# Mask added by TensorE for all head pairs, and P transposed by two transfers a pair

## The chip, the cores and the metric

The kernel runs on one core of a Trainium2 chip. The core has a matrix engine (TensorE, PE in the profile), three engines that work on elements (VectorE or DVE, ScalarE or ACT, GpSimd or POOL) and SyncE (SP), which here only issues transfers. All of them run side by side; each works through its own list of instructions in order, and an instruction starts when the semaphores it waits for have been raised. Matmul results land in PSUM, in banks of 128 x 512 numbers of 32 bits; everything else lies in SBUF, 128 partitions wide. The metric is the time of one execution on the device in microseconds; less is better.

## The reference

An attention with a forgetting gate is followed by a gated feed-forward network (FFN). There are 8 batches and 8 heads, 576 tokens, head size 64; the FFN takes 4608 tokens of 512 numbers to 1536 and back.

```python
scores = q @ k.T / sqrt(64)                       # per batch and head, 576 x 576
cum    = cumsum(log(clip(f, 1e-4, 1)))            # per batch and head, 576
scores = where(j > i, -1e9, scores + cum[i] - cum[j])
attn   = softmax(scores) @ v
x      = attn, heads side by side                 # 4608 x 512
out    = (silu(x @ w_gate) * (x @ w_val)) @ w_out
```

Since `cum[i]` is the same for a whole row, the softmax does not need it. The kernel computes `t = cum[j] - q.k/8` and takes `exp(min(t) - t)`; a masked place needs a very large `t`.

## The kernel before, in words

**Tiling.** The two heads of a pair are worked on together; there are 32 pairs, 0 to 31, four to a batch. A pair's 576 queries are cut into nine blocks of 64, and block `i` of both heads fills the 128 partitions (`qz` holds the queries with zeros in the other head's half). Block `i` sees only keys 0 to 64(i+1), so its row has 64(i+1) columns. Blocks 0 to 3 are group `g = 0`, blocks 4 to 8 group `g = 1`. The score rows are packed into banks (`BANKS`): two for group 0, five for group 1. A unit of work is a pair and a group.

**Stages of a unit.** (1) `load_pair` loads k, q and `cb` (the row `cum` of each head, spread over 64 partitions), `prepare` casts k and q on GpSimd, transposes them on TensorE (L447) and copies them out of PSUM (L459, L461). (2) `scores` multiplies a bank's rows on TensorE (L493) into one of two PSUM buffers `sp`. (3) VectorE adds `cb` to a row and writes `t`, and takes the least of the row in the same instruction; a second small instruction reads that least out into `tm` (all L517). (4) ScalarE takes the exponential with its row sum (L532). (5) VectorE turns row sums into factors `lr` (L546 to L550), GpSimd multiplies each row by its factor and packs it as 16-bit slices of 128 keys into `pk` (L568): 6 slices for group 0 and 19 for group 1. (6) The slices are transposed into `pT`. For pairs 0 to 7 (`ON_PE`) TensorE does that (L598), with copies out of PSUM (L603); for pairs 8 on, one transposing transfer issued by SyncE (L581) takes all 25 slices when both groups are packed (`joint`). (7) `weighted` multiplies by v on TensorE (L624); from pair 8 on it does both groups at once and waits for both halves of `pT`. The result is copied into `xT` (L648).

**The mask.** Only the last 64 columns of a row (the block against its own keys) need a mask. For pairs below `MFROM = 12`, TensorE adds it: one more matmul of 64 columns a row adds `mask` through the identity into the score bank (L497). For pairs 12 on, a copy `cm = cb + mask` of a pair is made first by GpSimd or VectorE (L476), and a row's add on VectorE is split in two: the earlier columns with `cb`, the last 64 with `cm`. The second piece starts from the least of the first, which it reads from `tm`.

**The FFN.** Tokens are cut into tiles 0 to 11 of 256, 256, seven times 512, 256, 128 and 128. `gate` multiplies by the two input matrices on TensorE (L706), ScalarE takes a tanh (L712), VectorE makes the product (L714, L717); `project` multiplies by the output matrix (L734), ScalarE or VectorE copies (L741, L743), SyncE stores (L746). In four PSUM buffers `gv` the FFN shares space with the transposes of P.

**What sets the order.** `Plan.order` goes through all operations before the program is written: each has costs by engine, what it reads and writes, and a priority. At each step the operation that can start first by these costs is placed on an engine, ties going to the lower priority number. So the costs, the latencies, the number of buffers in each pool, and the priorities fix the order of each engine's list; nothing is reordered at run time except what the engines do themselves. Attention units have low numbers (`at[p, g]`, the place in `ORDER`), the FFN's matmuls 1000 and more, so FFN work goes where attention cannot start. `NUDGE` adds to the priority of single units: `a` a unit of attention, `q` the preparation of a pair, `v` a batch's v, `f` and `o` a tile's gate and projection. `WAIT` makes an operation count as starting later by so many ns. SyncE's list holds all loads, transposing transfers and stores in that order, so one that waits holds up those behind it.

Of the kernel before, what the change touches and what calls it, by code (L numbers as in the profile page):

```python
# [14 lines left out]
BIG = 1.0e9  # L15
HUGE = 3.0e38
COLD = 25000


class Op:  # L20
# [11 lines left out]
class Plan:  # L32
# [29 lines left out]
    def order(self):  # L62
# [72 lines left out]
        while ready:  # L135
            best = None
            for n, r in ready.items():
                o = self.ops[n]
                got = room(o, r)
                if got is None:  # L140
                    continue
                for e, dur in o.engs.items():
                    s = max(r, got[0], free[e])
                    for k in o.reads:
                        if k in using and using[k][0] != e:
                            s = max(s, using[k][1])
                    c = (s + o.bias.get(e, 0), o.prio, n, e, dur, got[1])
                    if best is None or c[:4] < best[:4]:
                        best = c
            if best is None:  # L150
                raise RuntimeError("no operation can start: " + ", ".join(str(self.ops[n].writes) for n in list(ready)[:20]))
            s, _, n, e, dur, take = best
            o = self.ops[n]
            s -= o.bias.get(e, 0)
            if e == "PE" and s < COLD:
                dur *= 2
            for k, b in take:
                name = self.home[k]
                self.where[k] = b
                slots[name][b] = k  # L160
                taken[name, self.line[k]] += 1
            o.start, o.eng = s, e
            free[e] = s + dur
            for k in o.reads:
                if self.home.get(k) in self.banks:
                    using[k] = e, s + dur + 30
            if o.dma:
                q = e == "POOL"
                at = max(wire[q], s + (2550 if q else 2000))
                both = max(0, min(2 * o.dma, wire[not q] - at))  # L170
                wire[q] = at + o.dma + both / 2
                wire[not q] += both / 2
                if o.ring:
                    free[e] = max(free[e], wire[q] - 1450)
                o.end = wire[q] + 1100
            else:
                o.end = free[e] + o.lat
            for k in {*o.writes, *o.reads, *o.holds}:
                left[k] -= 1
                until[k] = max(until[k], o.end)  # L180
            del ready[n]
            for kid in kids.get(n, ()):
                waiting[kid.n] -= 1
                if not waiting[kid.n]:
                    ready[kid.n] = max(d.end for d in kid.deps)
            done.append(o)
# [10 lines left out]
def kernel(  # L197
# [36 lines left out]
             [[(8, 0, 512)], [(8, 512, 576), (6, 0, 448)], [(7, 0, 512)], [(5, 0, 384)], [(4, 0, 320)]]]  # L234


    MFROM = 12
    CMENG = ("POOL", "DVE")

    ON_PE = {(p, g) for p in range(8) for g in range(2)}  # L240

    NDIRECT = 0
    NSEL = 1
    MOST = (("p", 1), ("o", 2), ("f", 3))
# [11 lines left out]
    HEAD = "10 00 20 30 11 01 31 21"  # L256


    NUDGE = "a21.0:1 a31.1:10 f5:1 f7:4.5 o8:2 q11:-2 q15:4 q24:2.5"

    WAIT = ""
    ORDER = [(int(u[0]), int(u[1])) for u in HEAD.split()]
    ORDER += [(p, g) for p in range(len(ORDER) // 2, NPAIR) for g in (1, 0)]
    at = {u: n for n, u in enumerate(ORDER)}
# [30 lines left out]
    for i in range(0, NB, 2):  # L295
        bufs(f"e{i}", [P, QB * (i + 2)], F32, 2)
    bufs("eo", [P, 512], F32, 4)
    bufs("tm", [P, NB + 1], F32, 6)
    bufs("ls", [P, NB, 2], F32, 6)
    bufs("lr", [P, NB], F32, 6)  # L300
    both = {}
    for n in ("pk", "pT"):
        both[n] = [sb.tile([P, sum(NSL), P], BF16, name=f"{n}{x}") for x in range(2)]
# [114 lines left out]
    def prepare(p):  # L418
        s = first[p]
        for name in ("k", "q"):  # L420
# [4 lines left out]
            def cast(e, name=name, fk=fk, bk=bk, KR=KR):  # L425
# [5 lines left out]
                    eng[e].tensor_scalar(dst, src, -scale, 1.0, op0=ALU.mult, op1=ALU.mult)  # L431
                else:
                    eng[e].tensor_copy(dst, src)
            engs = {"POOL": 850}
            if p < NPB:
                engs = {"POOL": 850, "ACT": 850, "DVE": 500} if name == "k" else {"POOL": 1050, "ACT": 1050, "DVE": 680}
            o = pl.op(engs, cast, [fk], [bk], s - 1 + (name == "q") * .1)
# [30 lines left out]
    def copies(p):  # L468

        if p < MFROM:  # L470
            return
        pl.key(("cm", p), "cm")

        def add(e):
            src = pl.buf(("cb", p)).rearrange("r (i c) -> r i c", c=QB)
            eng[e].tensor_tensor(pl.buf(("cm", p)), src, maskf.unsqueeze(1).to_broadcast((P, NB, QB)), op=ALU.add)  # L476
        cost = {"POOL": S * 1.05 + 245, "DVE": S / .96 + 82}
        pl.op({e: cost[e] for e in CMENG}, add, [(("cb", p), 3)], [("cm", p)], first[p] - .5, holds=[("cb", p)])

    def scores(p, g):  # L480
        s = at[p, g]
        pl.key(("tm", p, g), "tm")
        pl.key(("ls", p, g), "ls")
        for n, bank in enumerate(BANKS[g]):
            sk = ("sp", p, g, n)
            pl.key(sk, "sp")
            pr = s + n * .05

            def mult(e, bank=bank, sk=sk):
                sp, kt, qz, o = pl.buf(sk), pl.buf(("kt", p)), pl.buf(("qz", p)), 0  # L490
                for i, a, z in bank:
                    last = z == QB * (i + 1)
                    nc.tensor.matmul(sp[:, o:o + z - a], qz[:, i, :, :].rearrange("p h r -> p (h r)"), kt[:, a:z],  # L493
                                     start=True, stop=not last or p >= MFROM)
                    o += z - a
                    if last and p < MFROM:
                        nc.tensor.matmul(sp[:, o - QB:o], ident, mask, start=False, stop=True)  # L497
            cols = [z - a for _, a, z in bank] + [64 for i, a, z in bank if z == QB * (i + 1) and p < MFROM]
            pl.op({"PE": mm(*cols)}, mult, [("kt", p), ("qz", p), (("kt", p), "done"), (("qz", p), "done"), "mask"], [sk], pr, lat=220)
            o = 0  # L500
            cuts = []
            for i, a, z in bank:
                last = z == QB * (i + 1)
                if last and a < QB * i and p >= MFROM:
                    cuts += [(i, a, QB * i), (i, QB * i, z)]
                else:
                    cuts.append((i, a, z))
            for i, a, z in cuts:
                last = z == QB * (i + 1)
                own = last and p >= MFROM  # L510
                tk = ("t", p, i)
                if a == 0:
                    pl.key(tk, "t")

                def add(e, i=i, a=a, z=z, o=o, sk=sk, tk=tk, last=last, own=own):
                    tm = pl.buf(("tm", p, g))
                    nc.vector.tensor_tensor_reduce(  # L517
                        out=pl.buf(tk)[:, a:z], in0=pl.buf(sk)[:, o:o + z - a],
                        in1=pl.buf(("cm", p))[:, i, :] if own else pl.buf(("cb", p))[:, a:z], scale=1.0,
                        scalar=HUGE if a == 0 else tm[:, NB:NB + 1], op0=ALU.add, op1=ALU.min,  # L520
                        accum_out=tm[:, i:i + 1] if last else tm[:, NB:NB + 1])
                w = [tk, ("tm", p, g)] + ([("m", p, i)] if last else [("m", p, i, "part")])
                r = [sk] + ([("cm", p)] if own else [(("cb", p), 3)]) + ([("m", p, i, "part")] if a else [])
                pl.op({"DVE": (z - a) / .96 + (142 if a else 82)}, add, r, w, pr, lat=100, holds=[] if own else [("cb", p)])
                o += z - a
                if last:
                    ek = ("e", p, i)
                    pl.key(ek, epool(i))

                    def exp(e, i=i, tk=tk, ek=ek):  # L530
                        L = QB * (i + 1)
                        nc.scalar.activation(pl.buf(ek)[:, :L], pl.buf(tk)[:, :L], AF.Exp,  # L532
                                             bias=pl.buf(("tm", p, g))[:, i:i + 1], scale=-1.0,
                                             accum_out=pl.buf(("ls", p, g))[:, i, 0:1])
                    sums[p, g] = pl.op({"ACT": QB * (i + 1) * .833 + 290}, exp, [tk, ("m", p, i)], [ek, ("ls", p, g)],
                          pr, lat=150, holds=[("tm", p, g)])

    def normalize(p, g):
# [10 lines left out]
        pl.op({"DVE": 95, "ACT": 200}, guard, [("ls", p, g)] + ([("z", "ls", n) for n in range(6)] if p < 3 else []), [("lr", p, g)], s, lat=120)  # L549
        pl.op({"DVE": 95}, lambda e: nc.vector.reciprocal(lr(), lr()), [("lr", p, g)], [("l2", p, g)], s, lat=170, holds=[("lr", p, g)])  # L550
        kk = ("pk", p, g)
        joint = not any((p, x) in ON_PE for x in range(2))
        pl.key(kk, f"pk{g}", same=("pk", p, 1 - g) if joint else None)
        w = HI[g] - LO[g] + 1
        for i in range(HI[g], LO[g] - 1, -1):
# [75 lines left out]
    def spread(p, g, pv):  # L631
# [5 lines left out]
        for a, z in ((0, cut), (cut, w)):  # L637
# [3 lines left out]
            def evac(e, a=a, z=z):  # L641
# [5 lines left out]
                src = bass.AP(src.tensor, src.offset + QB * (z - a - 1), [full[0], [-QB, z - a], full[2]])  # L647
                (nc.scalar.copy if e == "ACT" else nc.vector.tensor_copy)(dst, src)  # L648
            tok = t0 + a * QB, t0 + z * QB
            o = pl.op({"ACT": QB * (z - a) * .833 + 130, "DVE": QB * (z - a) / .96 + 85}, evac, [xk],  # L650
                      [("x", hp, n) for n in range(tok[0] // QB, tok[1] // QB)], s)
            o.bias = LATER if p >= 8 else {}
            evacs.append((pv, tok))
# [1 line left out]
    def load_v(b):  # L655
        for c in range(5):
# [9 lines left out]
                (), [fk], s, dma=1460 if n == P else 800, after=wait)  # L666
            def cast(e, c=c, n=n, fk=fk):
                (nc.scalar.copy if e == "ACT" else eng[e].tensor_copy)(pl.buf(("vt", b))[0:n, c, :, :], pl.buf(fk)[0:n, :, :])
            o = pl.op({"POOL": 670} if b else {"POOL": 670, "ACT": 580, "DVE": 600}, cast,
                  [fk] + ([("z", "vt", b)] if c == 4 and b < 2 else []), [("vt", b), ("vt", b, c)], s + .5)  # L670
            o.bias = SPARE

# [183 lines left out]
```

## Time and profile before

| | |
|---|---|
| median of 3 runs | 425.94 us (425.29 to 428.68) |
| profiled execution | 422.99 us |
| its span, first to last instruction | 421.1 us |
| granted TensorE clock | 1.000 |
| TensorE busy in the first 40 us, and from 400 to 420 us | 24.56 us, 17.87 us |
| transfers | 72.21 MB, mean 171 GB/s |

The profile gives, for one execution, each engine's busy time, the same in 40 equal slices, the chain of work that ended last, the costliest groups of instructions by source line, and who waited for whom. A busy TensorE is not the same as a TensorE at its peak: matmuls are pipelined, so one that shows as 0.38 us long can be followed by the next after 0.22 us. What counts is the distance from start to start. "Idle before" names what ended an idle time; it counts from the modelled end of the instruction before.

### The profile page before, as it was taken

How to read it: one execution, taken by the hardware profiler on the slowest of the kernel's cores; microseconds unless marked ns; L12 is line 12 of the kernel's file. 1: busy time of each engine (PE TensorE's matmuls, PEld its weight loads, DVE VectorE, ACT ScalarE, POOL GpSimd, SP SyncE). 2: the span in 40 equal slices, each digit the busy share in tenths (PEclk: the TensorE clock that was granted, in tenths of full speed). 3: DMA queues.
4: the chain of work that ended last, by engine and by line, in shares of the span. 5: the costliest groups of instructions: out<-in, count | busy, mean ns of one | idle time of the engine just before them, and what ended most of it. 6: DMA issues, size and time to landing. Idle time of an engine off the chain costs nothing.

```text
span 421.1 us, 10007 instructions
## 1 busy us (share of the span) xinstructions
PE 397.9 (94%) x3124; PEld 226.6 (54%) x3124; DVE 349.9 (83%) x1329; ACT 318.6 (76%) x882; POOL 269.3 (64%) x468
## 2 busy tenths in 40 slices
PE   2579999999999999999999999999999999999996
PEld 1446888665555555444544455454544444457675
DVE  4699999989998999899998999899989972765132
ACT  4599999999987989878998898798897843332221
POOL 7399978999985968767798696777964630000000
PEclk9999999999999999999999999999999999999999
DMA  7999999997999999999897999989948234000121
GB/s 199 197 151 248 213 213 208 230 233 181 203 205 198 262 189 225 225 247 190 175 228 187 235 208 214 221 193 188 224 113 166 57 85 115 2 25 27 51 76 50
DMA packets 143029, 72.21 MB, mean 171 GB/s; under 512 B 117760, under 2 KB 129792, under 8 KB 142976
## 3 DMA queue, kind: packets, MB, share of 16 engines
q1 hardware_dynamic: 136804, 66.27, 72.4%
q0 software_dynamic: 5808, 4.72, 7.5%
q10 hardware_dynamic: 364, 0.59, 0.5%
q8 instruction: 24, 0.39, 0.4%
q14 instruction: 29, 0.24, 0.2%
HBM read 47.04 MB, written 9.58 MB: 134 GB/s over the span
## 4 chain that ended last, share of the span: by engine, by line
PE 65%; DVE 18%; ACT 4%; issue 4%; DMA 4%; POOL 3%; SPq 0%; DVEq 0%; ACTq 0%; POOLq 0%
PE gv L706 33%; PE gv L734 16%; DVE t L517 10%; PE sp L493 7%; PE tx L624 4%; DMA qf<-in_q_dram 3%; DVE th L714 3%; PE tx L447 3%; DVE hh L717 3%; PE gv L598 2%; POOL pk L568 2%; ACT e L532 1%; ACT eo L532 1%; DVE qz L461 1%; DVE tm L517 1%
## 5 line engine op out<-in xcount | busy, mean ns | idle before, releaser
L568 POOL TENSOR_SCALAR pk<-e,lr 128x512 bf16<-128x512 f32 (+3 forms) x190 | 104.3, 552 | 55.6 <-issue 15.5
L517 DVE CUSTOM_DVE_ANT_0 t<-sp,cb 128x320 f32<-128x320 f32 (+7 forms) x268 | 121.0, 461 | 12.8 <-PE sp L493 1.7
L706 PE MATMUL gv<-xT,wv 128*128 128x512 bf16 (+2 forms) x576 | 111.2, 326 | 0.7 <-DVE th L714 0.6
L706 PE MATMUL gv<-xT,wg 128*128 128x512 bf16 (+2 forms) x576 | 111.4, 326 | 0.0
L734 PE MATMUL gv<-wo,hh 128*128 128x512 bf16 (+1 forms) x444 | 105.2, 373 | 0.0
L532 ACT ACTIVATE e<-t,tm 128x64 f32<-128x64 f32 (+4 forms) x160 | 88.6, 555 | 10.5 <-DVE tm L517 9.8
L714 DVE SCALAR_TENSOR_TENSOR th<-th,gv 128x512 f32<-128x512 f32 x108 | 73.8, 683 | 26.5 <-ACT th L712 25.8
L712 ACT ACTIVATE th<-gv 128x512 f32<-128x512 f32 x108 | 63.6, 590 | 32.5 <-PE gv L706 30.9
L532 ACT ACTIVATE eo<-t,tm 128x256 f32<-128x256 f32 (+3 forms) x128 | 71.3, 558 | 15.5 <-DVE tm L517 13.4
L493 PE MATMUL sp<-kt,qz 128*128 128x448 bf16 (+4 forms) x320 | 73.3, 293 | 6.6 <-DVE tm L517 5.8
L717 DVE TENSOR_TENSOR hh<-th,gv 128x512 bf16<-128x512 f32 x108 | 73.8, 684 | 4.2 <-PE gv L706 1.3
L568 POOL TENSOR_SCALAR pk<-eo,lr 128x256 bf16<-128x256 f32 (+3 forms) x128 | 68.2, 533 | 6.7 <-DVE tm L517 3.3
L706 PEld LDWEIGHTS <-wv 128*128 128x128 bf16 x576 | 50.6, 98 | 38.1 <-issue 3.6
L706 PEld LDWEIGHTS <-wg 128*128 128x128 bf16 x576 | 50.4, 98 | 36.8 <-issue 0.6
L734 PEld LDWEIGHTS <-hh 128*128 128x128 bf16 x444 | 41.0, 98 | 40.2 <-issue 1.0
L493 PEld LDWEIGHTS <-qz 128*128 128x128 bf16 x320 | 30.6, 100 | 27.3 <-issue 5.2
L517 DVE CUSTOM_DVE_ANT_0 t<-sp,cm,tm 128x64 f32<-128x64 f32 x160 | 42.2, 278 | 2.1 <-PE sp L493 0.2
L741 ACT ACTIVATE ot<-gv 128x512 f32<-128x512 f32 (+1 forms) x33 | 19.0, 578 | 25.5 <-PE gv L734 25.0
L517 DVE DVE_READ_ACCUMULATOR2_ANT tm<- 128x1 f32 x460 | 38.1, 83 | 0.0
L431 POOL TENSOR_SCALAR qb<-qf 72x1024 bf16<-72x1024 f32 x30 | 31.2, 1040 | 6.2 <-DMA qf<-in_q_dram 5.3
L459 ACT COPY qz<-tx 64x576 bf16<-64x576 bf16 x46 | 28.9, 628 | 3.5 <-PE tx L447 3.0
L532 ACT ACTIVATION_READ_ACCUMULATOR e<-t,tm 128x1 f32 x160 | 30.5, 191 | 0.0
(64 smaller groups left out, 403.1 us busy)
## 6 DMA issues: line engine op xcount, KB each, us to landing
out_dram<-ot SPq DMA_DIRECT2D x35, 256.0 KB
kf<-in_k_dram SPq DMA_DIRECT2D x31, 288.0 KB
qf<-in_q_dram SPq DMA_DIRECT2D x31, 288.0 KB
cb<-cum_f SPq DMA_DIRECT2D x62, 144.0 KB
vf<-in_v_dram SPq DMA_DIRECT2D x32, 256.0 KB
wo<-in_moe_w_out_dram POOLq DMA_DIRECT2D x3, 512.0 KB, 10.8
vf<-in_v_dram SPq DMA_DIRECT2D x8, 128.0 KB
wv<-in_moe_w_val_dram POOLq DMA_DIRECT2D x2, 512.0 KB, 7.6
```

The lines of the kernel that those rows point to most:

```text
L431: eng[e].tensor_scalar(dst, src, -scale, 1.0, op0=ALU.mult, op1=ALU.mult)
L459: nc.scalar.copy(dst, src)
L493: nc.tensor.matmul(sp[:, o:o + z - a], qz[:, i, :, :].rearrange("p h r -> p (h r)"), kt[:, a:z], start=True, stop=not last or p >= MFROM)
L517: nc.vector.tensor_tensor_reduce(out=pl.buf(tk)[:, a:z], in0=pl.buf(sk)[:, o:o + z - a], in1=pl.buf(("cm", p))[:, i, :] if own else pl.buf ...
L532: nc.scalar.activation(pl.buf(ek)[:, :L], pl.buf(tk)[:, :L], AF.Exp, bias=pl.buf(("tm", p, g))[:, i:i + 1], scale=-1.0, accum_out=pl.buf(( ...
L568: eng[e].tensor_scalar(dst, src, r, 1.0, op0=ALU.mult, op1=ALU.mult)
L706: nc.tensor.matmul(pl.buf(bk)[:, j * n:j * n + n], wt[:, ko, fc * P:fc * P + P], xT[:, ko, x0:x0 + n], start=ko == 0, stop=ko == KD - 1)
L712: pl.op({"ACT": 487}, lambda e, u=u: nc.scalar.activation(pl.buf(("th", t, u)), pl.buf(("wg", t, u)), AF.Tanh, scale=0.5), [("wg", t, u)], ...
L714: pl.op({"DVE": 605}, lambda e, u=u: nc.vector.scalar_tensor_tensor(pl.buf(("th", t, u)), pl.buf(("th", t, u)), 1.0, pl.buf(("wg", t, u)), ...
L717: pl.op({"DVE": 605}, lambda e, u=u: nc.vector.tensor_mul(pl.buf(("hh", t, u)), pl.buf(("th", t, u)), pl.buf(("wv", t, u))), [("u", t, u), ...
L734: nc.tensor.matmul(pl.buf(bk)[:, 0:z - a], hh[:, (fc % nf) * n + ms * P:(fc % nf) * n + ms * P + P], wo[:, fc, a:z], start=fc == 0, stop=f ...
L741: nc.scalar.mul(pl.buf(ok)[:, a:z], pl.buf(bk)[:, 0:z - a], 0.5)
```

## The change

`MFROM` goes from 12 to 32, so all pairs add their mask on TensorE: `cm` is never built, and no row is split at its last 64 columns. `JFROM = 32` takes the place of the test on `ON_PE`: no pair is joint any more, and from pair 8 on each group has a transposing transfer of its own, of 19 and of 6 slices. `lr` has 5 buffers in place of 6. `tm` has another layout, with the same content for these pairs. Several costs by which the order is planned are set anew (VectorE's by 3% after 100 us of the plan, GpSimd's casts, ScalarE's copies, a latency), and `NUDGE` and `WAIT` name more units. With `TWO` a branch is added that pairs from `MFROM` on would take; with `MFROM = 32` no pair takes it. `HEAD`, the order of the first units, stays.

```diff
 COLD = 25000
+SLOW = 1.03
...
             if e == "PE" and s < COLD:
                 dur *= 2
+            if e == "DVE" and s > 100000:
+                dur *= SLOW
...
-    MFROM = 12
+    MFROM = 32
...
+    JFROM = 32
+    TWO = True
...
-    NUDGE = "a21.0:1 a31.1:10 f5:1 f7:4.5 o8:2 q11:-2 q15:4 q24:2.5"
-
-    WAIT = ""
+    NUDGE = "a11.0:1 a12.0:1.5 a14.0:0.5 a15.0:-0.5 a15.1:0.5 a16.0:2 a17.0:-0.5 a19.0:-2.5 a21.0:1 a22.0:-2 a23.0:2 a24.1:4 a25.0:-2 a26.0:2 a28.1:2 a31.1:10 f5:1 f7:8.5 f9:-7 o8:2 o9:-1 q11:-2 q15:3 q24:2.5 q25:-0.5 v6:10.5 v7:12"
+
+    WAIT = "f8:200"
...
-    bufs("tm", [P, NB + 1], F32, 6)
+    bufs("tm", [P, 2, NB], F32, 6)
     bufs("ls", [P, NB, 2], F32, 6)
-    bufs("lr", [P, NB], F32, 6)
+    bufs("lr", [P, NB], F32, 5)
...
-            engs = {"POOL": 850}
+            engs = {"POOL": 850 if p < 8 else 800 if name == "k" else 1010}
...
-                pl.op({"DVE": (z - a) / .96 + (142 if a else 82)}, add, r, w, pr, lat=100, holds=[] if own else [("cb", p)])
+                pl.op({"DVE": (z - a) / .96 + (142 if a and not two else 82)}, add, r, w, pr, lat=100 if p < 8 else 140, holds=[] if own else [("cb", p)])
...
-        joint = not any((p, x) in ON_PE for x in range(2))
+        joint = p >= JFROM
...
-            o = pl.op({"ACT": QB * (z - a) * .833 + 130, "DVE": QB * (z - a) / .96 + 85}, evac, [xk],
+            o = pl.op({"ACT": QB * (z - a) * .833 + (130 if p < 8 else 50), "DVE": QB * (z - a) / .96 + 85}, evac, [xk],
...
-            o = pl.op({"POOL": 670} if b else {"POOL": 670, "ACT": 580, "DVE": 600}, cast,
+            o = pl.op({"POOL": 670 if b < 2 else 590} if b else {"POOL": 670, "ACT": 580, "DVE": 600}, cast,
```

With `joint` false, a pair from 8 on takes this branch, which the kernel before has too and did not use:

```python
        if (p, g) not in ON_PE:
            pl.op({"SP": 300 + 153 * NSL[g]}, lambda e: nc.sync.dma_start_transpose(
                out=pl.buf(tk), in_=pl.buf(kk).rearrange("p s k -> p (s k)")),
                [kk], [tk], s - 1, dma=500 + 118 * NSL[g]).ring = True
            return
```

## The prediction

> **What bounds the kernel now.** I read the page first, then the busy time by stretch, the chain, and the waits of TensorE.
>
> ```profile
> span 421.1 us, 10007 instructions
> ...
> PE 397.9 (94%) x3124; PEld 226.6 (54%) x3124; DVE 349.9 (83%) x1329; ACT 318.6 (76%) x882; POOL 269.3 (64%) x468
> ...
> PE   2579999999999999999999999999999999999996
> ...
> DVE  4699999989998999899998999899989972765132
> ...
> PEclk9999999999999999999999999999999999999999
> ```
>
> ```profile
> 0.00:40.00 40.00, 24.56 (x222) 17.63 (x223) 29.03 (x108) 29.10 (x81) 29.62 (x73) 1.00 1.00 196
> 40.00:120.00 80.00, 79.52 (x841) 54.83 (x839) 77.22 (x266) 77.56 (x217) 72.43 (x120) 1.00 1.05 214
> 120.00:340.00 220.00, 215.93 (x1487) 107.21 (x1484) 205.58 (x900) 187.58 (x542) 163.70 (x271) 1.00 0.93 196
> 340.00:418.00 78.00, 77.87 (x582) 46.96 (x580) 38.03 (x58) 24.04 (x45) 3.51 (x6) 1.00 0.15 47
> ```
>
> In the second view the columns after the stretch and its length are busy time of PE, PEld, DVE, ACT and POOL. Two engines look full from 40 to 340 us: TensorE and VectorE. They are not full in the same way. VectorE stops mattering at 340 us; TensorE goes on without a hole to the end. The chain says how:
>
> ```profile
> 343.93 6.91 PE gv L734 x32
> 350.83 0.81 PE tx L624 x14
> ...
> 355.20 17.27 PE gv L706 x80
> ```
>
> 32 matmuls of 512 columns in 6.91 us, 80 in 17.27: one takes a **slot** of 0.216 us (0.42 ns a column and little more), back to back. So what is done earlier shortens the last stretch, and what is added on TensorE anywhere lengthens the span by its slot. The kernel's time is the start, plus TensorE's slots, plus TensorE's holes. VectorE matters only through the holes:
>
> ```profile
> PE sp L493 <- DVE tm L517: 2.0, 8, 0.4
> PE gv L706 <- DVE th L714: 0.6, 2, 0.3
> PE tx L447 <- ACT xT L648: 0.4, 1, 0.4
> PE tx L447 <- POOL qb L431: 0.4, 1, 0.4
> ```
>
> These are TensorE's waits from 120 to 345 us: scores wait until VectorE has emptied one of the two score banks. They understate the loss, because a matmul's modelled end hides the start of a hole:
>
> ```profile
> 284.05 1.03 PE L706 MATMUL gv<-xT,wg 128*128 128x512 bf16 x4
> 285.48 0.38 PE L493 MATMUL sp<-kt,qz 128*128 128x512 bf16 x1 [0.41 <-DVE tm L517]
> ```
>
> Four slots from 284.05 end at 284.91; the score starts at 285.48. The hole is 0.57 us, of which 0.41 is shown: 0.16 is hidden.
>
> **How large are the holes where the change acts?** From below: 220 - 215.93 = 4.07 us idle, plus 0.16 for each of the 12 waits, 6.0 us. From above I count slots from 120 to 340 us; these are the first four and the last of 18 rows by shape:
>
> ```profile
> L706 PE MATMUL gv<-xT,wg 128*128 128x512 bf16 x243 | 62.6, 379 | 0.0
> L706 PE MATMUL gv<-xT,wv 128*128 128x512 bf16 x240 | 61.6, 379 | 0.6 <-DVE th L714 0.6
> L734 PE MATMUL gv<-wo,hh 128*128 128x512 bf16 x240 | 59.6, 379 | 0.0
> L493 PE MATMUL sp<-kt,qz 128*128 128x512 bf16 x40 | 15.2, 379 | 0.8 <-DVE tm L517 0.4
> ...
> L624 PE MATMUL tx<-pT,vt 128*64 128x64 bf16 x44 | 4.3, 193 | 0.0
> ```
>
> 763 matmuls of 512 columns x 0.216 = 164.8; 22 weighted groups (44 matmuls of 64 columns, two a group) x 0.81 from the chain = 17.8; smaller scores by their columns 15.9, transposes of k and q 9.4. Together 207.9, so 12.1 us at most are holes. I take 9, midway.
>
> **Mask on TensorE for pairs 12 to 31.** By the order of instructions this adds 180 mask matmuls (108 become 288), each with a weight load. Masked pairs stand in the trace already:
>
> ```profile
> 112.16 0.19 PE L497 MATMUL sp<-mask,ident 128*128 128x64 bf16 x1
> 112.18 0.35 PE L493 MATMUL sp<-kt,qz 128*128 128x448 bf16 x1
> 112.37 0.19 PE L497 MATMUL sp<-mask,ident 128*128 128x64 bf16 x1
> 112.40 1.03 PE L706 MATMUL gv<-xT,wv 128*128 128x512 bf16 x4
> ...
> L497 PEld LDWEIGHTS <-ident 128*128 128x128 bf16 x108 | 10.6, 103 | 6.1 <-issue 3.7
> ```
>
> A mask starts, and the next matmul starts 0.02 to 0.03 us later; it shows 0.19 because of its tail. At 0.029 (64 columns), 180 cost **5.2 us**, all on the path. The 0.10 us weight loads vanish in neighbouring slots.
>
> The Trainium skill speaks against this price. "TensorE: Matmul & The Clock Gate", section "Back-to-back issue gap", says that in a stream of weight loads and matmuls a 128-column matmul is spaced at about 81 ns, since columns alone leave out the load. By that figure 180 masks would be an estimated 14.6 us. The trace, with 0.03 us between starts, disagrees here.
>
> On VectorE 140 split adds go, each with its accumulator read (460 reads become 320), and 12 builds of the masked copy; on GpSimd 8 builds:
>
> ```profile
> L517 DVE CUSTOM_DVE_ANT_0 t<-sp,cm,tm 128x64 f32<-128x64 f32 x160 | 42.2, 278 | 2.1 <-PE sp L493 0.2
> ...
> L517 DVE CUSTOM_DVE_ANT_0 t<-sp,cb 128x512 f32<-128x512 f32 x44 | 30.0, 681 | 0.1
> ...
> L517 DVE CUSTOM_DVE_ANT_0 t<-sp,cb 128x448 f32<-128x448 f32 x32 | 19.8, 617 | 1.7 <-ACT lr L546 0.2
> ...
> L476 POOL TENSOR_TENSOR cm<-cb,maskf 128x576 f32<-128x576 f32 x8 | 11.3, 1409 | 0.0
> ...
> L476 DVE TENSOR_TENSOR cm<-cb,maskf 128x576 f32<-128x576 f32 x12 | 10.3, 859 | 0.2
> ...
> 284.05 0.28 DVE L517 CUSTOM_DVE_ANT_0 t<-sp,cm,tm 128x64 f32<-128x64 f32 x1
> 284.26 0.08 DVE L517 DVE_READ_ACCUMULATOR2_ANT tm<- 128x1 f32 x1
> 284.26 0.16 DVE L548 TENSOR_REDUCE lr<-ls 128x5 f32<-128x10 f32 x1
> ```
>
> A split add holds VectorE from 284.05 to 284.26, 0.21 us; 64 more columns in the add before it cost 0.681 - 0.617 = 0.064. So 140 x 0.146 = 20.4 us, and 10.3 for the copies: **30.7 us less** out of 205.6 from 120 to 340 us. By the order VectorE gets five output copies and five copies of k from ScalarE, about 7 us. GpSimd loses 11.3. None of this is on the path by itself. It counts as shorter holes, since a bank is emptied sooner.
>
> How much shorter? The stretch 40 to 120 us has the mask on TensorE already, with VectorE at 77.22 of 80, and only 0.48 us idle. Over 220 us that rate is 1.3 instead of 4.07: a third remains. So of 9 us some 3 stay and **6.1 go**. The holes that stay are single late arrivals.
>
> **Two transfers of P a pair.** Weighted sums of pairs 8 on still wait for both halves, so the larger transfer started early removes no wait of TensorE by itself:
>
> ```profile
> L581 SPq DMA_TRANSPOSE pT<-pk x24: 3722/4223/5323, 101.5 to 344.3; - x24
> ...
> PEld L624 <- DMA pT<-pk: 0.4, 1, 0.4
> ```
>
> 25 slices hold SyncE 3.7 to 5.3 us, 0.15 to 0.21 a slice; 19 take then 2.9 and 6 take 0.9 at the low rate. The only wait of TensorE on this transfer is 0.4 us, so at most 0.4 is to be won. The loss has no row: 24 more issues on SyncE, each standing ahead of loads and outputs behind it. Its bounds: nothing, if they lie in SyncE's waits for GpSimd; 24 x 0.4 = 9.6 us, if each weighted group met that one recorded wait. I take 0, the value of 23 of the 24 pairs now, and keep 9.6 as a rival.
>
> **Placing.** Up to TensorE's row 1783 of 6244, matmul 890, the order is the same: about 100 us by the counts of the stretches (222 up to 40 us, 841 in the next 80). The start, 15.4 of 40 us idle, stays. Before the last score bank stand 233 FFN groups of 0.86 us in the old order and 236 in the new: attention does not end earlier. Between that bank and the last weighted sum stand 15 groups and one weighted sum, now 14 groups and three: 13.8 us of cover against 14.5. GpSimd has the five upper rows of the last pair left in both. The first row after it needs a 19-slice transfer in place of 25. So the end keeps its cover, and I put the placing at 0; the sixth buffer of row sums goes at 0 too, as no wait names its release. Holes from placing are inside the 9 us.
>
> **Sum.** 421.1 + 5.2 - 6.1 = 420.2 us of span. The profiled execution took 422.99, 1.9 more than its span; the median of three runs is 425.94, another 2.95 more. I carry the difference of -0.9 to the median: **425.0 us**.
>
> **Rivals.**
> - *All holes close.* With 30.7 us off VectorE nothing but the mask remains: 12.1 of holes gone, -6.9, **419.0 us**. For it: most named waits point at VectorE. Against: the planner puts scores as early as a bank comes free, so relief is spent on a tighter order, and late ScalarE and GpSimd results stay.
> - *No hole closes.* The new order is as tight as the old; TensorE pays the mask alone: +5.2, **431.1 us**, slower. It decides as soon as fewer than 0.9 us of holes go (then over 1% slower). For it: 236 against 233 groups, no earlier end. Against: the 40 to 120 us stretch.
> - *P comes late.* SyncE stands at a transfer whose GpSimd rows are not done, and loads, outputs and the second half queue behind. 0.4 us at each of 24 weighted sums: +5.2 - 6.1 + 9.6 = +8.7, **434.6 us**. It decides from 0.22 us a pair. Against: one wait of 0.4 in all now.
> - *The weight load is not hidden.* If each mask needs the 0.103 us of its load, 180 x 0.103 = 18.5 in place of 5.2: **438.3 us**. That is the skill's rule as a mechanism of this kernel; 0.03 us between starts speaks against it.
> - *The change doesn't do what it says:* the six-slice transfer lands after where the joint one did, because it waits for the same last GpSimd row, and nothing moves. That leaves the forecast's 425.0.
>
> **How the numbers follow.** Forecast, with the last case, 0.58; all holes close 0.13; no hole closes 0.15; P late 0.11; load not hidden 0.03. A measurement of this kernel can tell about 1%, 4.3 us, from no change: under 421.7 is faster, over 430.2 slower. Faster: 0.13 and an edge of the forecast, 0.15. Slower: 0.11 + 0.03 and two thirds of "no hole closes", 0.24. Same: 0.61. The range reaches from the first rival's 419.0 over the unrecovered mask's 431.1 to 431.5, and leaves out the late transfers and the unhidden load, 0.14.
>
> **What the profile after would show.** Mask: 288 at L497's counterpart with starts 0.03 us apart. VectorE: about 24 us less busy. Holes: TensorE's wait for VectorE before scores under 1 us after 120 us, and idle near 1.3 of 220. Transfers: 48, near 2.9 and 0.9 us, no wait of weighted sums. The last 60 us again full. I am wrong if weighted sums wait for transfers, if TensorE waits for the FFN's own VectorE results, or if the first 100 us move.

## The result, and the profile after

The changed kernel takes 422.18 us (median of 17 runs, 418.83 to 425.69) against 425.92 us for the kernel before in the same sessions (423.69 to 429.64). The ratio is 0.9891, with a 95% interval of 0.9863 to 0.9919: 1.1% faster, some 4.6 us. The ratio leaves out three executions of the changed kernel that took over 425.1 us; between the medians of all 17 lie 3.7 us. The forecast was 425.0 us, 0.9 less than before: the sign held, and the gain is four to five times as large.

The profiled execution of the changed kernel took 423.56 us, of which 421.8 is its span: longer than the profiled 421.1 of before. It holds a disturbance at 41 us, described below, that the profiled execution of before does not have, so the two spans must not be compared as they are; the stretches after 50 us can be. First the page after, in the same rows as before: span, busy time, and TensorE, VectorE and TensorE's granted clock in 40 slices.

```profile
span 421.8 us, 10037 instructions
...
PE 399.4 (95%) x3304; PEld 232.6 (55%) x3304; DVE 325.3 (77%) x1045; ACT 312.4 (74%) x874; POOL 253.3 (60%) x460
...
PE   1578899999999999999999999999999999999996
...
DVE  4599599998999888968988887799967851876132
...
PEclk9999899999999999999999999999999999999999
```

VectorE is 24.6 us less busy (325.3 for 349.9); in the middle its row now shows 6, 7 and 8 beside the 9s. TensorE's row has a dip in slices 4 and 5, and the clock row an 8 in the fifth. By stretch (length, then busy time of PE, PEld, DVE, ACT, POOL, the granted clock, the transfers' share and GB/s):

```profile
0.00:40.00 40.00, 23.74 (x214) 16.89 (x215) 28.31 (x105) 28.25 (x80) 28.11 (x69) 1.00 0.96 185
40.00:120.00 80.00, 77.10 (x820) 53.69 (x818) 72.52 (x249) 73.53 (x205) 68.91 (x115) 0.98 0.98 206
120.00:340.00 220.00, 220.00 (x1682) 114.62 (x1680) 187.44 (x637) 185.11 (x543) 152.74 (x271) 1.00 0.99 198
340.00:418.00 78.00, 78.00 (x595) 47.13 (x592) 37.01 (x57) 25.10 (x48) 3.51 (x6) 1.00 0.21 56
```

From 120 to 340 us TensorE is busy **220.00 of 220 us**, where it was 215.93: the profile shows no idle time there any more. VectorE is at 187.44 instead of 205.58. TensorE's waits over the whole run are all at the start or at single places; for 120 to 345 us the view of waits has no row at all (the numbers of a row are us in all, times, and the longest wait):

```profile
PE tx L452 <- POOL kb L438: 8.5, 1, 8.5
PE sp L498 <- DVE tm L526: 3.5, 8, 1.1
...
PE tx L638 <- POOL vt L682: 1.4, 1, 1.4
PE gv L612 <- POOL pk L582: 1.3, 4, 0.4
```

No idle time shown is not the same as no hole, since a matmul's modelled end covers a short one. So the slots from 120 to 340 us are counted as the prediction did for the kernel before; these are the first five and the last of 19 rows by shape:

```profile
L720 PE MATMUL gv<-xT,wg 128*128 128x512 bf16 x256 | 65.8, 379 | 0.0
L720 PE MATMUL gv<-xT,wv 128*128 128x512 bf16 x254 | 65.5, 379 | 0.0
L748 PE MATMUL gv<-wo,hh 128*128 128x512 bf16 x240 | 60.2, 379 | 0.0
L502 PE MATMUL sp<-mask,ident 128*128 128x64 bf16 x186 | 29.8, 193 | 0.0
L498 PE MATMUL sp<-kt,qz 128*128 128x512 bf16 x40 | 15.1, 382 | 0.0
...
L638 PE MATMUL tx<-pT,vt 128*64 128x64 bf16 x40 | 3.9, 193 | 0.0
```

790 matmuls of 512 columns x 0.216 = 170.6; 20 weighted groups x 0.81 = 16.2; 186 masks x 0.029 = 5.4; smaller scores 16.4, transposes of k and q 9.5. Together 218.1, so 1.9 us at most are holes, where the same count left 12.1 in the kernel before. About 10.2 us of holes have gone. A count of the time beyond the slots in both traces, from each matmul's start to the next and with slots by columns alone, gives the same difference: 15.0 us before, 4.8 after.

The added matmuls (L502 in the rows above) in the timeline of TensorE (start, length, instruction):

```profile
200.66 0.19 PE L502 MATMUL sp<-mask,ident 128*128 128x64 bf16 x1
200.69 0.35 PE L498 MATMUL sp<-kt,qz 128*128 128x448 bf16 x1
200.87 0.19 PE L502 MATMUL sp<-mask,ident 128*128 128x64 bf16 x1
200.90 0.43 PE L452 MATMUL tx<-ident,qb 72*128 72x72 bf16 x8
```

0.03 us from the start of a mask to the next start, as in the masked pairs of before; from 130 to 340 us the median is 0.028. And the transfers, 48 for 24, of two sizes (23 took 1.2 to 1.9 us and 25 took 2.9 to 6.1, where 0.9 and 2.9 were expected):

```profile
L600 SPq DMA_TRANSPOSE pT<-pk x48: 1211/2867/6067, 104.5 to 345.8; - x48
```

The disturbance is in the timelines of GpSimd and TensorE, and in TensorE's busy time by stretches of 2 us (with the granted clock, the transfers' share and GB/s behind it):

```profile
42.26 0.61 POOL L682 CAST vt<-vf 128x512 bf16<-128x512 f32 x1 [2.86 <-DMA vf<-in_v_dram]
```

```profile
42.93 0.44 PE L638 MATMUL tx<-pT,vt 128*64 128x320 bf16 x6 [1.45 <-POOL vt L682]
```

```profile
42.00:44.00 2.00, 0.85 (x10) 1.00 1.16 280
44.00:46.00 2.00, 0.90 (x8) 1.00 1.04 228
46.00:48.00 2.00, 2.00 (x18) 0.61 0.83 131
48.00:50.00 2.00, 2.00 (x15) 0.54 1.16 184
50.00:52.00 2.00, 2.00 (x33) 1.00 1.13 302
```

A piece of v arrives 2.86 us late on GpSimd, TensorE is less than half full for 4 us, and then runs at 0.61 and 0.54 of its clock for 4 us (18 and 15 matmuls started, where a full 2 us has 33). The order of instructions is the same up to there in both kernels; the kernel before had its v in time in the profiled execution.

### The profile page after: what moved, and what is told of

It is laid out like the page before. It is cut to its first block, busy times and chain, and to the rows that moved or that the text cites. A ratio compares the mean times of both kernels' runs of the same rounds, so it can differ in the third digit from the quotient of the medians.

```text
span 421.8 us, 10037 instructions
## 1 busy us (share of the span) xinstructions
PE 399.4 (95%) x3304; PEld 232.6 (55%) x3304; DVE 325.3 (77%) x1045; ACT 312.4 (74%) x874; POOL 253.3 (60%) x460
## 4 chain that ended last, share of the span: by engine, by line
PE 87%; DMA 5%; POOL 3%; DVE 2%; issue 1%; ACT 1%; SPq 0%; POOLq 0%; DVEq 0%
PE gv L720 43%; PE gv L748 22%; PE sp L498 9%; PE tx L638 6%; PE tx L452 4%; DMA vf<-in_v_dram 2%; PE gv L612 2%; PE sp L502 2%; POOL pk L582 2%; DMA qf<-in_q_dram 2%; DMA kf<-in_k_dram 1%; DVE t L526 1%; POOL vt L682 1%; DVE qz L466 0%; POOL wv L695 0%
## 5 line engine op out<-in xcount | busy, mean ns | idle before, releaser
L526 DVE CUSTOM_DVE_ANT_0 t<-sp,cb 128x512 f32<-128x512 f32 (+7 forms) x288 | 130.8, 476 | 14.5 <-PE sp L502 7.6
L582 POOL TENSOR_SCALAR pk<-e,lr 128x512 bf16<-128x512 f32 (+3 forms) x190 | 100.6, 533 | 47.7 <-DVE lr L564 26.6
L546 ACT ACTIVATE e<-t,tm 128x320 f32<-128x320 f32 (+4 forms) x160 | 88.9, 557 | 9.1 <-DVE tm L526 7.0
L582 POOL TENSOR_SCALAR pk<-eo,lr 128x512 bf16<-128x512 f32 (+3 forms) x128 | 68.3, 534 | 20.9 <-DMA pT<-pk 6.2
L498 PE MATMUL sp<-kt,qz 128*128 128x64 bf16 (+7 forms) x320 | 72.7, 294 | 3.6 <-DVE tm L526 3.5
L546 ACT ACTIVATE eo<-t,tm 128x512 f32<-128x512 f32 (+3 forms) x128 | 71.1, 557 | 5.8 <-DVE tm L526 4.7
L502 PE MATMUL sp<-mask,ident 128*128 128x64 bf16 x288 | 47.8, 197 | 0.0
L502 PEld LDWEIGHTS <-ident 128*128 128x128 bf16 x288 | 27.1, 100 | 14.3 <-issue 3.5
L755 ACT ACTIVATE ot<-gv 128x512 f32<-128x512 f32 (+1 forms) x28 | 16.1, 578 | 24.1 <-PE gv L748 23.9
L638 PE MATMUL tx<-pT,vt 128*64 128x320 bf16 (+4 forms) x448 | 29.6, 266 | 1.6 <-POOL vt L682 1.4
```

The costliest lines, as they stand in the source:

```text
L526: nc.vector.tensor_tensor_reduce(out=pl.buf(tk)[:, a:z], in0=pl.buf(sk)[:, o:o + z - a], in1=pl.buf(("cm", p))[:, i, :] if own else pl.buf ...
L582: eng[e].tensor_scalar(dst, src, r, 1.0, op0=ALU.mult, op1=ALU.mult)
L638: nc.tensor.matmul(xo[r, 0:QB * n], vt[:, c, 2 * hp + h, :], pT[:, a:a + n, 64 * h:64 * h + 64], start=(c == 0), stop=(c == nch - 1))
```

## The experiments

Theory A: the mask on TensorE closes TensorE's holes because it relieves VectorE. Theory B: the new costs and the placing close them. Theory C: the two transfers do. Ratios are to the kernel before on the same chip, in brackets with 95% intervals; 0.01 is 4.3 us.

**Each part of the change alone.** The mask:

```diff
-    MFROM = 12
+    MFROM = 32
```

> The kernel before with MFROM = 32 and nothing else: all pairs take the mask on TensorE, one transfer a pair, old costs, old priorities. If the relief of VectorE closes the holes (theory A), TensorE's idle time from 120 to 340 us falls from 4.07 us to under 1.5 us, and the span changes by +5.2 for the masks less 6 to 9 of holes: -1 to -4 us. If the holes close through the costs or the placing (theory B), the idle time stays at 3 to 5 us and the span grows by 3 to 6 us. If the two transfers close them (theory C), the same as B.

0.9941 [0.9898, 0.9984], so 2.5 us faster, with order and priorities that were not made for it. TensorE's waits from 120 to 345 us are these ("issue" stands for records that are missing from this trace, so idle time is not read here):

```profile
PE tx L624 <- DMA pT<-pk: 2.2, 4, 0.9
PE tx L447 <- POOL qb L431: 1.1, 2, 0.6
PE tx L447 <- POOL kb L433: 0.5, 2, 0.3
PE sp L493 <- issue: 0.3, 2, 0.2
PE gv L706 <- issue: 0.2, 1, 0.2
```

The eight waits on VectorE are gone without new costs and new priorities. In their place weighted sums wait 2.2 us for the one transfer of 25 slices, which they had hardly done before. Theory A holds for the waits; in the one execution that was profiled (427.78 us, one of the longest of 12) a new wait has taken part of the gain.

The transfers:

```diff
-        joint = not any((p, x) in ON_PE for x in range(2))
+        joint = False
```

> The kernel before with joint = False from pair 8 on, and nothing else: two transfers a pair, of 19 and 6 slices, mask as before. Theories A and B: within 1.5 us of before, since weighted sums still wait for both halves; TensorE's waits on the transfer stay under 1 us. Theory C: 2 us or more faster. The rival of late P: 3 us or more slower, with TensorE waiting at weighted sums.

1.043 [1.0377, 1.0484], 18 us slower, which no theory had expected; theory C is refuted, as far as it means the transfers alone. Nor does P come late: no weighted sum waits for a transfer. From 120 to 345 us:

```profile
PE sp L493 <- DVE tm L517: 13.1, 24, 2.2
PE tx L624 <- DVE qz L461: 1.0, 1, 1.0
```

```profile
120.00:340.00 220.00, 201.18 (x1363) 100.39 (x1387) 198.51 (x841) 173.67 (x498) 155.44 (x256) 0.98 0.93 189
```

VectorE has nearly the same work as before (358.6 us busy over the whole run for 349.9), but in another order, and TensorE waits for it 24 times in place of 8. Eleven of these waits, 8.2 us, lie between 183 and 204 us. The granted clock in that stretch of 220 us is 0.98 (before 1.00), which is another 4 us or so by estimate (2% of 220); from 180 to 205 us it is 0.80. GpSimd waits 7.4 us for loads of k where it had waited 0.7, so it is not excluded that loads which stand behind the transfers have a part in it. The costs alone:

```diff
+            if e == "DVE" and s > 100000:
+                dur *= SLOW
...
-            engs = {"POOL": 850}
+            engs = {"POOL": 850 if p < 8 else 800 if name == "k" else 1010}
```

(and the other four costs of the change; one of them, for building `cm`, plays no part in the changed kernel, which builds none)

> The kernel before with the costs of the changed kernel (VectorE's 3% after 100 us, GpSimd's casts, ScalarE's copy, the latency of 140) and nothing else. Theory A: within 2 us of before, since VectorE has the same work and the same holes. Theory B: the order leaves room for a late VectorE, idle time of TensorE from 120 to 340 us under 2 us, and 2 to 6 us faster than before, without a mask to pay for.

1.0336 [1.0276, 1.0396], 14 us slower; TensorE waits 6.4 us for VectorE from 120 to 345 us (before: 2.0), and once 5.2 us for a transfer near the end. Theory B is refuted in its simple form: costs that are closer to the trace do not by themselves close a hole. With VectorE at 93% (205.58 of 220), an order that was not fitted to it loses 14 to 18 us in these two runs.

**The price of a mask.**

```diff
-                    if last and p < MFROM:
-                        nc.tensor.matmul(sp[:, o - QB:o], ident, mask, start=False, stop=True)
+                    if last:
+                        nc.tensor.matmul(sp[:, o - QB:o], ident, mask if p < MFROM else zero, start=False, stop=True)
```

> The kernel before with the 180 mask matmuls added for pairs 12 to 31 but with zeros in them, while the copies with the mask and the split adds stay: the price of the matmuls without their gain. If a mask takes a 0.029 us slot, +5.2 us (less what falls into holes that are there anyway, so +3 to +5.2); if its weight load of 0.10 us is not hidden, +13 to +18 us.

1.0264 [1.0215, 1.0313], 11 us. That is neither value: counting the matmuls in the plan moved the order as well. So the same matmuls once more, hidden from the plan, with the order of every engine unchanged but for them:

> The kernel before with 180 mask matmuls of zeros for pairs 12 to 31 that the plan does not count, so that every engine's order stays as it was: the price of the matmuls alone. By slots of 0.029 us: +5.2 us, less up to 2 us that fall into holes. If the weight load of 0.10 us is not hidden: +13 us and more. If the zero masks of the run before cost their 10 us by themselves: +10 us; if that was the new order, about +4.

1.013 [1.0082, 1.0178], +5.5 us [3.5, 7.6]. And the other way round, the changed kernel without them:

```diff
-                    if last and p < MFROM:
+                    if last and p < 12:
```

> The changed kernel without the mask matmuls of pairs 12 to 31, order as it is; left out is the mask of these pairs, so their softmax takes in later keys of the own block. If TensorE is the bound without holes, 180 slots of 0.029 us go: -5.2 us against the changed kernel, so about 417. If the matmuls lay in holes, under 2 us; if weight loads count, -13 us and more.

0.9774 [0.971, 0.9838], against 0.9891: 5.0 us less (by the two intervals some 2 to 8). Both agree with 180 slots of 0.029 us, 5.2 us, and with TensorE being the bound: what is added or taken there comes out one for one. The rest of the 11 us in the first of the three, some 6 us, was the order.

**The relief put back.** If VectorE's relief closes the holes, work put back on VectorE must open them, in the same order:

```diff
+                    if p >= 12 and last and 0 < i < 8:
+                        nc.vector.tensor_copy(pl.pools["cm"][0][:, 0, :], maskf)
```

> The changed kernel, order as it is, with 140 copies of 64 columns put behind the merged adds of pairs 12 to 31 on VectorE (about 20 us, what the change took off). Theory A (relief of VectorE closes the holes): the waits for VectorE come back, TensorE's idle time from 120 to 340 us goes from 0 to 3 us or more, +3 to +9 us against the changed kernel, so 426 to 431. Theory B (the costs and the placing close them): under 2 us slower than the changed kernel.

1.0232 [1.0167, 1.0296] against 0.9891, 14.5 us slower. From 120 to 345 us:

```profile
PE sp L498 <- DVE tm L526: 6.4, 13, 2.3
PE gv L722 <- DVE th L730: 2.3, 2, 2.0
```

The waits are back, but the dose was wrong:

```profile
L532 DVE COPY cm<-maskf 128x64 f32<-128x64 f32 x134 | 44.9, 335 | 0.0
```

These copies lasted 0.335 us in the mean instead of the 0.14 planned. So the kind of add that the change had taken away, on the same score bank, was put there:

```diff
+                    if p >= 12 and last and 0 < i < 8:
+                        nc.vector.tensor_tensor_reduce(
+                            out=pl.pools["cm"][0][:, i, :], in0=pl.buf(sk)[:, o + z - a - QB:o + z - a],
+                            in1=pl.buf(("cb", p))[:, z - QB:z], scale=1.0, scalar=HUGE, op0=ALU.add, op1=ALU.min,
+                            accum_out=tm[:, 1, i:i + 1])
```

> The changed kernel, order as it is, with 140 adds of 64 columns from the score bank put back behind the merged adds of pairs 12 to 31 (the kind of work that the change took off VectorE, 0.14 us each, about 20 us; the copies of the run before lasted 0.335 us each, 44.9 us, and so were twice the dose). Theory A (relief closes the holes): waits for VectorE before scores return, TensorE's idle time from 120 to 340 us goes from 0 to 2 us or more, 3 to 8 us slower than the changed kernel, a ratio of 0.997 to 1.008. Theory B (costs and placing alone): within 2 us of the changed kernel, a ratio of 0.985 to 0.994.

0.9945 [0.9908, 0.9981], 2.3 us slower than the changed kernel, with four waits for VectorE from 120 to 345 us, 1.0 us in all as shown, where there were none. The expectation is missed: the ratio lies between the ranges given for the two theories, and its interval overlaps that of the changed kernel. Records of TensorE are missing here too, so idle time isn't read. With the large dose it is clear that VectorE's load opens holes; with the small one the sign is right, and the size, 2.3 us, is less than the holes that the change closed. An order that was made for less load may absorb some of it; no run shows that.

**Costs, placing, transfers, given the mask.** The changed kernel with the old priorities:

```diff
-    NUDGE = "a11.0:1 a12.0:1.5 ... v6:10.5 v7:12"
-    WAIT = "f8:200"
+    NUDGE = "a21.0:1 a31.1:10 f5:1 f7:4.5 o8:2 q11:-2 q15:4 q24:2.5"
+    WAIT = ""
```

> The changed kernel with NUDGE and WAIT of the kernel before: mask, transfers and costs stay, the placing of later units goes. Theory A: a few us slower than the changed kernel at most (422 to 427), with no waits for VectorE before scores. If the placing carries the gain: 428 and more, with waits named at transfers, casts or VectorE.

0.9996 [0.9951, 1.0041]: 4.5 us are lost, although from 120 to 345 us TensorE waits only 1.6 us for VectorE and 0.6 us for ScalarE. The profiled execution of this run has the late v too (4.0 us of TensorE's wait), so that the trace can't say where all of the 4.5 lie. Eleven of its 12 executions have a granted clock under 0.999, against seven of 17 of the changed kernel. The changed kernel with the old costs:

> The changed kernel with the costs of the kernel before (no 3% on VectorE, old casts, copies and latency); mask, transfers and priorities stay. If the new costs matter by themselves, 3 us or more slower than the changed kernel, with waits at casts of q and k or at scores. If any order that the priorities were not set for loses some us, the same, but with the waits at single places.

1.005 [1.0009, 1.009]: 6.8 us are lost, 3.6 of them shown as four waits for VectorE, the longest 1.9 (here ten of 12 executions have a clock under 0.999). And the kernel before with mask and transfers only, old costs and old priorities:

```diff
-    MFROM = 12
+    MFROM = 32
...
-        joint = not any((p, x) in ON_PE for x in range(2))
+        joint = False
```

> The kernel before with the mask on TensorE for all pairs and two transfers a pair; old costs, old priorities. Against the mask alone (ratio 0.994, 2.2 us of waits of weighted sums on the one transfer): if the two transfers take these waits away and bring nothing else, 1 to 3 us faster than the mask alone, a ratio of 0.987 to 0.992. If they only shift the order, a ratio of 0.992 to 1.003, and waits on transfers of over 1 us stay.

0.9901 [0.9861, 0.994]. Its waits from 120 to 345 us:

```profile
PE tx L447 <- POOL qb L431: 0.7, 2, 0.4
PE sp L493 <- DVE tm L517: 0.7, 2, 0.4
PE gv L706 <- issue: 0.2, 1, 0.2
PE sp L493 <- issue: 0.2, 1, 0.2
```

The waits for the transfer, 2.2 us with the mask alone, are gone, and the ratio is 0.4% lower; the intervals of the two overlap, so the size rests on the waits. Mask and transfers give what the whole change gives, as far as the intervals can tell (0.9901 and 0.9891), and they do so with the old costs and priorities, which speaks against theory B more plainly than the costs alone did. Among executions with a clock of 0.999 or 1.000 the medians are 422.4 us here (seven of eight) and 420.6 for the whole change (ten of 17), on different chips, so up to 2 us may yet belong to costs and priorities. These belong together: each without the other loses 4 to 7 us, part of which may be the lower clock.

**The late v.** One load earlier in SyncE's list, into a buffer of its own, all other orders as they are:

```diff
+        pl.pools["vf"].append(third)
+        pl.where["vf", 0, 2] = 2
+        ops.remove(loads["v", 0, 2])
+        ops.insert(ops.index(loads["cb", 4, 0]), loads["v", 0, 2])
```

> The changed kernel, order of the engines as it is, with one load of v (batch 0, keys 256 to 383) put five places earlier in SyncE's list, ahead of a load of cum, into a buffer of its own. If the late v at 41 us is what makes TensorE wait and takes its granted clock down to 0.88 in that stretch, both go, the runs come closer together and the median falls 2 to 4 us below the changed kernel, a ratio of 0.980 to 0.985. If the late v is only one sign of loaded transfers, another wait takes its place between 35 and 50 us and the ratio stays within 0.003 of 0.989.

0.9865 [0.9815, 0.9915], 420.38 us (419.23 to 424.01). In its trace the wait is gone and the clock stays (36 to 50 us, and 120 to 340 us):

```profile
36.00:50.00 14.00, 13.54 (x165) 11.16 (x164) 13.20 (x38) 13.71 (x35) 13.96 (x23) 1.00 1.17 234
```

```profile
120.00:340.00 220.00, 220.00 (x1681) 114.36 (x1678) 186.11 (x631) 184.18 (x541) 152.05 (x268) 1.00 0.99 197
```

The span is 417.5 us. But one trace is not all executions. Of the 17 of the changed kernel, ten have a granted clock of 0.999 or 1.000 on record and took 418.83 to 422.27 us, and seven have 0.996 or less and took 423.09 to 425.69. With the earlier load four of six are of the first kind (419.23 to 420.82) and two of the second (422.31 and 424.01, clock 0.996 and 0.995). So the earlier load does not keep the clock in every execution, and what lowered it in those two no trace shows. The direction is as expected, the size is not settled: 0.0026 below the changed kernel, with overlapping intervals, just above the range given. It is the fastest of the complete kernels here by its median, and its profile is the one to set beside that of before, since neither has a late v.

## Why the prediction was right or wrong

- **TensorE is the bound; a slot added is a slot longer.** Right, shown both ways: +5.5 us for 180 zero masks in the old order, -5.0 us without the masks in the new.
- **A mask costs 0.029 us, 5.2 us in all.** Right. The rival of the weight load (18.5 us) falls with the same two runs, as does the 14.6 us that stood beside the Trainium skill, "TensorE: Matmul & The Clock Gate", section "Back-to-back issue gap". Its other formula there, columns over 2.4 and 2.5 ns, gives an estimated 29 ns, and here the trace agrees.
- **VectorE 24 us less busy.** Right: 24.6.
- **Holes of 6.0 to 12.1 us, taken as 9.** The bounds held, the value was too small. The same count of slots gives 12.1 us before and 1.9 after, so 10.2 us went, and +5.2 - 10.2 = -5.0 us lies within what was measured (3.4 to 5.8 less, by the interval of the ratio). The lower bound of 6.0 was too low for a reason: it added 0.16 us to each of the 12 waits that the view names, but a hole that ends within a matmul's modelled tail is in no view. From start to start the trace before has, in this stretch and without the weighted sums, 67 distances that are over 0.03 us longer than the slot; after the change there are 22. The spans with the late v out of the way, 417.5 against 421.1, differ by 3.6 us; in these two single executions the first matmul also starts 0.7 us later (8.46 for 7.78).
- **A third of the holes stays, 6.1 go.** This is the step that failed: idle from 120 to 340 us is 0.00 in the changed kernel, not 1.3, and by slots about a sixth of the holes stays, 1.9 of 12.1. I had scaled from the stretch 40 to 120 us, where the mask was on TensorE already. But there VectorE was at 77.22 of 80 us (97%), as it also copied P out of PSUM. The change left it at 187.44 of 220 (85%). I took a stretch that was alike in the operation and not in the load; that the load makes the difference fits these numbers and was not tested by itself. The rival "all holes close" was nearer than the forecast: 10.2 of its 12.1 went.
- **The transfers are worth 0.** Wrong with the mask in place, and for a reason that I had not in view: with the mask alone weighted sums began to wait 2.2 us for the joint transfer. With the two transfers that wait is gone; the times of the two runs alone (0.9941 and 0.9901, overlapping intervals) do not settle the size. The row of 0.4 us that I used is of the order before; it says nothing on how late P is once VectorE is faster. That a split alone costs 18 us had no place in my rivals either; the late P that I feared did not come to the weighted sums.
- **Placing and costs are worth 0.** Right as a sum to within some 2 us; hidden in it are two parts of 4 to 7 us against each other.
- **The first 100 us do not move.** Right for the order; but in the profiled execution the first 50 us lose time to the late v. The order of before meets it as well: in the trace with the hidden zero masks TensorE waits 1.2 us for v at that place, with the clock at 1.00. How many executions of each kernel meet it is not known.
- **The range, 419.0 to 431.5,** holds the median 422.18; the forecast of 425.0 lies 2.8 above it. That the range reaches so low is owed to the rival "all holes close" and not to the sum. The gain of 1.09% by the ratio is just beyond the 1% that I had set for a change that can be told from none, a case that I had given 0.15; the median itself lies 0.5 us above the 421.7 that I had named.

What stays open: how much of the 4.5 us that the old priorities cost lies in the late v, and why the order that the plan makes for the transfers alone fits VectorE so much worse. The work is nearly the same, so the order is the likely cause; which of its steps, and what part the later loads have, is not shown. Open is also what lowers the clock in some executions with the earlier load of v.

## What to carry to other kernels

Where one engine is full to the end, count its slots from start to start: work added there can be priced from two rows, and any other engine matters only through the holes that it makes. Count these holes from start to start as well, since idle time in the profile shows only what outlasts a matmul's modelled end. Before scaling holes from another stretch of the same trace, compare the load of the engine that makes them, not only the operation. A part of a change tried alone, with the order planned anew, measures the order as well; hide the added work from the plan, and the price comes out clean.

## What the runs showed of the hardware that was not expected

**The granted clock after holes.** After 4 us at less than half load at 42 to 46 us the clock was 0.61 and 0.54 for 4 us, then 1.00 again. In the run with the split adds put back it was 0.60 from 44 to 46 us and 0.50 from 46 to 50. In the run with the copies TensorE was as empty (0.54 and 0.94 us busy of 2 from 42 to 46 us), and the clock stayed at 1.00:

```profile
42.00:44.00 2.00, 0.54 (x7) 1.00 1.16 283
44.00:46.00 2.00, 0.94 (x6) 1.00 1.13 270
46.00:48.00 2.00, 1.74 (x23) 1.00 0.85 140
```

Counted from start to start, TensorE loses 4.1 us beyond its slots from 40 to 50 us in the run with the copies and 5.5 in the changed kernel, against 1.0 in the kernel before. The Trainium skill, "TensorE: Matmul & The Clock Gate", section "What's actually happening", says that the gate looks at activity in windows of about 3.4 us that run freely; that would make it a matter of where the hole falls, and the two cases fit that. No run here moved the hole to test it.

**Copies from SBUF to SBUF on VectorE.** 140 copies of 64 columns lasted 0.179 us at least, 0.190 in the median and up to 2.398, while adds of the same width that read PSUM and SBUF lasted 0.211 to 0.222:

```profile
L532 DVE COPY cm<-maskf x140: 179/190/2398, 129.5 to 355.5; 128x64 f32<-128x64 f32 x140
```

```profile
L532 DVE CUSTOM_DVE_ANT_0 cm<-sp,cb x140: 211/220/222, 131.2 to 345.1; 128x64 f32<-128x64 f32 x140
```

The Trainium skill, "SBUF — State Buffer", section "SBUF: two separate sides", names a port pair that VectorE and GpSimd share and that one instruction holds to its end; GpSimd was at work in that stretch (143.62 us busy from 120 to 340 us), and the long copies fit. That GpSimd held the port in each of them was not looked at.
